# Attention with squared ReLU, then a feed-forward block, on one core: the first q and k in fp32 on SyncE's queue with a cast on chip, a TensorE warm-up, batch 1's first transposes on ScalarE, and batch 1's centering per feature block from PSUM

## The chip, the cores and the metric

The kernel runs on one core of one Trainium2 chip. The metric is the device time of one execution in microseconds (us). Most executions of one kernel repeat within 0.3%, but the times of this kernel and its variants fall into groups about 1.2 us (0.2%) apart, and telling these groups apart is half of this study. "Clock" is the share of TensorE's full clock that the chip granted, as the profile records it; a half-clock window is a stretch of 3.413 us (or two of them) at a clock of 0.5. All runs quoted are of the state "fast", or single runs whose state can't be told ("unknown", said where it is so).

Engines: PE = TensorE matmul, PEld = its weight loads, DVE = VectorE, ACT = ScalarE, POOL = GpSimd, SP = SyncE.

## The reference, cut to what matters

```python
# q, k, v: (batch 8, heads 12, seq 448, head_dim 64), fp32
scores = q @ k.T / sqrt(64)                       # per batch and head
attn   = maximum(scores, 0) ** 2 / 448
x      = (attn @ v), heads joined: (8, 448, 768)
# feed-forward with a layer norm ahead of it
xn  = (x - mean) / sqrt(var + 1e-6) * g_ln        # per row of 768
out = x + maximum(xn @ w_ch1, 0) @ w_ch2          # 768 -> 3072 -> 768
```

There is no softmax, so a score tile passes through three engines: TensorE makes it (called QK below), ScalarE or VectorE applies scale and ReLU, VectorE (or Pool) squares it, TensorE multiplies it with v (called AV).

## The kernel before: the parts that the change and the argument touch

Heads are taken in pairs of pairs: `n` counts groups of four heads ("pair n" in the texts), three of them (`NPER`) for each batch, and seven score tiles (`J`) in each. The kernel is emitted by a list scheduler that runs at build time: every piece of work is an `Op` with a guessed cost, and the guesses decide in which order each engine gets its instructions. On the chip the order of each queue is fixed. Loads go through Pool's software queue and are cast from fp32 to bf16 on the way:

```python
    nc.vector.memset(ones, 1.0 / d_model)
    ...
    with nc.allow_non_contiguous_dma(reason="768 gains, once"):
        nc.sync.dma_start(g_sb, moe_g_ln.rearrange("(ko kp) -> kp ko", kp=P))   # first of all loads

    def load_qk_rows(b, n):
        for t, src in enumerate((q, k)):
            ...
                nc.gpsimd.dma_start(stage[b][:, t, n::NPER, :], rows[:, n::NPER, :])
    ...
    with tc.manual_schedule():
        load_qk_rows(0, 0)
        ops["ident"] = R.add("POOL", 1300.0, lambda eng: make_identity(nc, identity), key=-1.0)
        load_qk_rows(0, 1)
        load_v(0)
        load_qk_rows(0, 2)
        load_qk_rows(1, 0)
        load_w1(0, 4)
        # ... the rest of batch 1 and of the weights
```

Batch 0 and 1 turn q and k by TensorE transposes into PSUM (the memory that matmuls write) and copy them to SBUF (the memory that matmuls read). In batch 0 each of q and k is one copy; batch 1's are one instruction of 1792 columns, on whichever engine the scheduler finds free:

```python
    def att_T(n):
        ...
        ev = R.add(("DVE", "ACT"), (1100.0, 1700.0), lambda eng: copy(
            eng, qkT[b][:, :, pn::NPER, :], st[0].rearrange("p t (j c) -> p t j c", c=P)), [op], key=0.01 * n - 0.008)
```

A score tile lives in a ring of nine buffers (`N_AT = 9`), which is freed tile by tile by AV. The squares are separate `Op`s for VectorE or Pool. When all three pairs of batch 0 are through AV, the means are taken by matmuls with a matrix of ones, and the first feed-forward can start after centering (VectorE) and gains (ScalarE), block by block:

```python
        mean_part(0)
        mean_part(1)
        mean_part(2)
        center(0)
        ...
        ffn_1_pair(0)
```

Batch 1 is centered otherwise: ScalarE copies the mean from PSUM to SBUF first, then four wide subtractions, then six gains, and only then does its first feed-forward matmul start.

## Time and profile before

| | before |
|---|---|
| time, median of six runs | 545.84 us (545.78 to 547.07) |
| PE busy of the profiled span (544.2 us) | 97% |
| PE busy in the first 5 us; first transposes | 0; at 5.40 us |
| first ReLU on ScalarE | 8.88 us |
| VectorE and ScalarE busy from 8.25 to 31 us (22.75 us) | 20.32 and 18.93 us |
| first AV matmul of pair 0 | 15.12 us |
| first subtraction of batch 0's centering | 30.79 us |

The head of the kernel, up to batch 0's centering, is the only place where PE waits for long.

The page of the kernel before (span; busy time and share of each engine):

```profile
span 544.2 us, 9868 instructions
PE 528.4 (97%) x4207; PEld 286.2 (53%) x4207; DVE 285.9 (53%) x494; ACT 227.8 (42%) x376; POOL 115.0 (21%) x133
```

The chain of waits of the kernel before, in order of time, its longer pieces up to 12 us (start, length, what the chain went through):

```profile
2.11 4.42 DMA t<-in_k_dram
6.57 0.97 PE ps L401 x16
7.57 0.63 DVE t L414
8.25 0.61 PE sc L466 x4
8.88 0.93 ACT a L475
9.85 0.58 PE sc L466 x3
10.44 1.34 PE ps L401 x49
```

The head begins with a load, and what follows is slow: four QK matmuls take 0.61 us here and 0.38 us later, which is TensorE at half clock.

The busy times in two stretches of the kernel before (busy time and count of each engine; then granted clock, DMA share, GB/s):

```profile
0.00:5.00 5.00, 0.00 (x0) 0.00 (x0) 0.22 (x2) 1.49 (x2) 3.88 (x11) 1.00 0.51 55
8.25:31.00 22.75, 18.51 (x365) 11.05 (x366) 20.32 (x37) 18.93 (x27) 12.20 (x16) 1.00 1.26 204
```

Five us with nothing on PE, then 22.75 us in which VectorE and ScalarE are both nearly full. The clock column says 1.00 although TensorE was cold: a record of the clock exists only from the first change on, here at 12.7 us, and time ahead of it counts as full.

The timeline of the kernel before (start, busy time, engine, line, operation; in brackets the idle time ahead and what ended it):

```profile
10.64 0.61 DVE L484 TENSOR_TENSOR a<-a 128x896 bf16<-128x896 bf16 x1
...
13.81 0.67 POOL L314 DMA_DIRECT2D v_t<-in_v_dram  x1 [1.35 <-DMA v_t<-in_v_dram]
...
15.12 1.52 PE L519 MATMUL ps<-a,v_t 64*64 64x448 bf16 x28
...
30.79 0.55 DVE L722 TENSOR_TENSOR a<-xT_e,ps 128x384 bf16<-128x384 bf16 x1
```

The first square is at 10.64. v comes in two halves, and AV needs both; "v" below is the second. It has landed by 13.81 (Pool's next load of v waited for it), 1.3 us before AV uses it. So v is early enough here, by a little.

### The profile page before, as it was taken

What the parts mean: (1) busy time and instruction counts of PE and PEld (TensorE: products, weight loads), DVE (VectorE), ACT (ScalarE), POOL (GpSimd) and SP (SyncE); (2) the same over time, 40 slices, a digit from 0 to 9 for tenths busy, and PEclk for the clock granted to TensorE, in tenths of its full rate; (3) what the DMA queues carried; (4) which work ended last, traced back from release to release, by engine and by line L of the source; (5) the groups of instructions that cost most, each with busy time, mean ns of one, the idle gap of its engine ahead of it and who ended that gap; (6) DMA issues with size and microseconds to landing.
All of it is one profiled execution on the core that took longest, in us unless ns stands there. A gap on an engine that the chain in (4) does not pass through costs nothing.

```text
span 544.2 us, 9868 instructions
## 1 busy us (share of the span) xinstructions
PE 528.4 (97%) x4207; PEld 286.2 (53%) x4207; DVE 285.9 (53%) x494; ACT 227.8 (42%) x376; POOL 115.0 (21%) x133
## 2 busy tenths in 40 slices
PE   4889999999999999999999999999999999999996
PEld 3444455555554455554555455555555555555563
DVE  3996566427864466834467355853456535540011
ACT  3976621115325653556124653265422554044200
POOL 7511700041270123410152120600210102100000
PEclk9999999999999999999999999999999999999999
DMA  9999999997199404990169601993023100510022
GB/s 144 205 200 180 211 170 145 158 149 143 41 157 149 69 1 83 160 158 1 31 87 183 117 1 34 167 145 55 2 51 82 30 0 1 96 50 1 1 58 59
DMA packets 141611, 51.36 MB, mean 94 GB/s; under 512 B 121728, under 2 KB 137344, under 8 KB 141568
## 3 DMA queue, kind: packets, MB, share of 16 engines
q0 software_dynamic: 81616, 25.96, 48.7%
q1 hardware_dynamic: 55472, 13.97, 19.7%
q10 hardware_dynamic: 4480, 10.82, 7.2%
q8 instruction: 33, 0.54, 0.4%
q14 instruction: 10, 0.08, 0.0%
HBM read 51.91 MB, written 11.01 MB: 116 GB/s over the span
## 4 chain that ended last, share of the span: by engine, by line
PE 94%; DVE 3%; ACT 1%; DMA 1%; issue 0%; POOL 0%; ACTq 0%; POOLq 0%
PE o_ps L838 40%; PE ps L782 40%; PE sc L466 6%; PE ps L519 5%; DVE a L484 1%; PE ps L401 1%; DMA t<-in_k_dram 1%; ACT a L710 1%; DVE t L414 1%; ACT a L475 1%; DVE a L477 0%; PE slot L681 0%; DVE xT_e L534 0%; DVE o_t L852 0%; ACT xT_e L532 0%
## 5 line engine op out<-in xcount | busy, mean ns | idle before, releaser
L782 PE MATMUL ps<-a,w 128*128 128x448 bf16 x1140 | 221.5, 353 | 0.0
L838 PE MATMUL o_ps<-w,h 128*128 128x384 bf16 x1200 | 199.7, 326 | 0.0
L782 PEld LDWEIGHTS <-w 128*128 128x128 bf16 x1140 | 108.8, 98 | 108.8 <-issue 10.6
L838 PEld LDWEIGHTS <-h 128*128 128x128 bf16 x1200 | 116.1, 98 | 81.5 <-issue 5.5
L475 ACT ACTIVATE a<-sc 128x896 bf16<-128x896 f32 x109 | 96.7, 925 | 93.2 <-PE sc L466 89.4
L797 ACT ACTIVATE h<-ps 128x448 bf16<-128x448 f32 (+1 forms) x161 | 85.1, 529 | 106.4 <-PE ps L782 105.9
L477 DVE TENSOR_SCALAR a<-sc 128x896 bf16<-128x896 f32 x59 | 64.1, 1087 | 108.4 <-PE sc L466 108.3
L484 DVE TENSOR_TENSOR a<-a 128x896 bf16<-128x896 bf16 x168 | 105.9, 669 | 3.6 <-ACT a L475 3.4
L852 DVE SCALAR_TENSOR_TENSOR o_t<-o_ps,r_t,a 128x384 f32<-128x384 f32 x56 | 34.4, 615 | 106.8 <-PE o_ps L838 106.5
L466 PE MATMUL sc<-t 64*64 64x448 bf16 x672 | 48.5, 365 | 3.5 <-ACT a L475 2.1
L519 PE MATMUL ps<-a,v_t 64*64 64x448 bf16 x672 | 37.8, 351 | 0.9 <-DVE xT_left L534 0.4
L710 ACT ACTIVATE a<-a,g_sb 128x448 bf16<-128x448 bf16 x38 | 22.3, 657 | 26.0 <-DVE a L703 21.6
L466 PEld LDWEIGHTS <-t 64*64 64x64 bf16 x672 | 18.0, 107 | 26.2 <-issue 19.6
L519 PEld LDWEIGHTS <-v_t 64*64 64x64 bf16 x672 | 19.9, 107 | 15.2 <-issue 4.0
L330 POOL DMA_DIRECT2D t<-in_q_dram x12 | 19.3, 1773 | 30.0 <-DMA t<-t 28.4
L604 POOL TENSOR_TENSOR sum_t<-sum_t,xT_o 128x384 f32<-128x384 f32 x7 | 6.4, 913 | 87.3 <-ACT xT_o L532 74.2
L838 PE MATMUL o_ps<-w,t 128*128 128x384 bf16 x144 | 23.9, 326 | 0.0
L330 POOL DMA_DIRECT2D t<-in_k_dram x12 | 23.7, 2527 | 0.0
L604 POOL TENSOR_TENSOR sum_t<-sum_t,xT_e 128x384 f32<-128x384 f32 x6 | 5.5, 912 | 81.1 <-ACT xT_e L532 76.0
L314 POOL DMA_DIRECT2D v_t<-in_v_dram x16 | 17.9, 1495 | 14.6 <-PE ps L782 6.6
L602 POOL TENSOR_TENSOR sum_t<-xT_o 128x384 f32<-128x384 bf16 x4 | 3.6, 910 | 80.9 <-DVE a L484 66.0
L838 PEld LDWEIGHTS <-t 128*128 128x128 bf16 x144 | 13.9, 98 | 9.8 <-issue 0.7
(60 smaller groups left out, 216.7 us busy)
## 6 DMA issues: line engine op xcount, KB each, us to landing
out_dram<-o_t ACTq DMA_DIRECT2D x54, 192.0 KB, 2.9
v_t<-in_v_dram POOLq DMA_DIRECT2D x16, 336.0 KB, 17.0
w<-in_moe_w_ch_dram POOLq DMA_DIRECT2D x4, 1152.0 KB, 41.8
t<-in_q_dram POOLq DMA_DIRECT2D x12, 336.0 KB, 7.6
t<-in_k_dram POOLq DMA_DIRECT2D x12, 336.0 KB, 11.7
w<-in_moe_w_ch_dram POOLq DMA_DIRECT2D x4, 768.0 KB, 15.7
w<-in_moe_w_ch_dram POOLq DMA_DIRECT2D x1, 1536.0 KB, 29.7
t<-in_q_dram POOLq DMA_DIRECT2D x6, 224.0 KB, 8.7
```

Source lines behind the costliest of these rows:

```text
L314: nc.gpsimd.dma_start(vt[b][half * T:(half + 1) * T], v[b, half * 6:half * 6 + 6].rearrange("h (p j) d -> p h (j d)", j=J))
L330: nc.gpsimd.dma_start(stage[b][half * T:(half + 1) * T, t].rearrange("p j (h d) -> p j h d", d=D), src[b, half * 6:half * 6 + 6].rearrange ...
L466: nc.tensor.matmul(sc[rows_of(half), r, :S], qkT[b][rows_of(r), 1, s * NPER + pn, rows_of(half)], qT[:, :, pn, rows_of(half)], start=True, ...
L475: nc.scalar.activation(attn[n, s], st[0][:, :, :S], Act.Relu, scale=rc2)
L477: nc.vector.tensor_scalar(attn[n, s], st[0][:, :, :S], rc2, 0.0, op0=Alu.mult, op1=Alu.max)
L484: nc.vector.tensor_mul(attn[n, s], attn[n, s], attn[n, s])
L519: nc.tensor.matmul(av_st[n][half][rows_of(hh)], vt[b][rows_of(half), 2 * pn + hh, s * D:(s + 1) * D], attn[n, s][rows_of(half), hh, :], st ...
L710: nc.scalar.mul(o, o, g_sb[:, ki:ki + 1])
L782: nc.tensor.matmul(ps, w1[:, ki, ni * P:(ni + 1) * P], xc[b][:, ki, :], start=(i == 0), stop=(i == K1 - 1))
L797: nc.scalar.activation(o, st[0][:, c], Act.Relu)
L838: nc.tensor.matmul(o_st["ps"], stat(ki), w2[:, ki, j * hd:(j + 1) * hd], start=(ki == 0), stop=(ki == K2 - 1))
L852: nc.vector.scalar_tensor_tensor(o_st[u, m][:, j * hd:(j + 1) * hd], ps, rstd[b][:, ri:ri + 1], xm[u, m][:, j * hd:(j + 1) * hd], op0=Alu. ...
```

## The change

The intent: start the head sooner and keep TensorE warm. Six things change (the code is cut; "..." marks what is left out).

1. The first q and k come over SyncE's hardware queue in three pieces (q, three sevenths of k, the rest of k), as fp32, and are cast on VectorE or ScalarE. The 768 gains, which led all loads, now follow these pieces.
2. 36 dummy matmuls warm TensorE up while it waits.
3. Batch 1's first transposes (pair 3) are copied by two instructions of 896 columns, on ScalarE only.
4. The mean matmuls enter the stream of AV pieces, so that pairs 0 and 1 are summed before pair 2 is evacuated; squares of batch 1 are held until batch 0 is centered.
5. Batch 1 is centered block by block from PSUM like batch 0, and its first feed-forward is cut into six parts.
6. The scheduler's bookkeeping follows (`flat`, `ahead`, `hold`).

```diff
+    FIRST = ((0, 0, J), (1, 0, 3), (1, 3, J))
+
+    def load_first():
+
+        raw = {}
+        ops["qk_ld", 0, 0] = []
+        for i, (t, j0, j1) in enumerate(FIRST):
+            cols = slice(j0 * D, j1 * D)
+            ... # i == 0: raw[0] is an fp32 view of a buffer that batch 1 uses later
+                nc.sync.dma_start(raw[0][:, t, :, cols], rows[:, 0::NPER, cols])
+            ld = R.add("SP", 480.0, emit, [], key=float(i), load=(2 * P, 22.0 + 7.0 * (j1 - j0)))
+
+            def cast(eng, t=t, cols=cols):
+                copy(eng, stage[0][:, t, 0::NPER, cols], raw[0][:, t, :, cols])
+            ops["qk_ld", 0, 0].append(
+                R.add(("DVE", "ACT"), (100.0 + 67.0 * (j1 - j0), 200.0 + 107.0 * (j1 - j0)), cast, [ld], key=-3.0))
 ...
+        if pn == 0:
+            ev = None
+            for t in range(2):
+                ev = R.add("ACT", 940.0, lambda eng, t=t: copy(
+                    eng, qkT[b][:, t, pn::NPER, :], st[0][:, t].rearrange("p (j c) -> p j c", c=P)), [op, ev], key=0.01 * n - 0.008)
+        else:
             ev = R.add(("DVE", "ACT"), (1100.0, 1700.0), ...)      # one copy, either engine
 ...
-        if n == NPER and s < 3:
+        if n == NPER and ("xc", 0) not in ops:
             held.append(add_square)
 ...
-        if b > 0:
+        if b > 1:
             sv = R.add("ACT", 560.0, save, [op, free], key=-2.0)   # mean to SBUF
 ...
-        if b == 0:
+        if b < 2:
             for ki in [pn + NPER * h for pn in range(NPER) for h in range(2)]:
                 ... # subtract one block from PSUM, then its gain
 ...
+        deps = f1_deps(b, ni)
+        for part in [[x] for x in k] if (b, ni) == (1, 0) else [k]:
+            op = R.pe(1135.0 / K1 * len(part), lambda eng, part=part: emit(eng, part), deps)
+            deps = [ops["xc", b][min(part[0][0] + 1, K1 - 1)]]
 ...
-        load_qk_rows(0, 0)
-        ops["ident"] = R.add("POOL", 1300.0, lambda eng: make_identity(nc, identity), key=-1.0)
+        ops["ident"] = R.add("POOL", 1300.0, lambda eng: make_identity(nc, identity), key=-2.0)
+        load_first()
+
+        def warm_up(eng):
+            ps = ps_s.tile([P, 2, 512], fp32, tag="s")
+            for i in range(N_WARM):                                # 36
+                nc.tensor.matmul(ps[:, 0, :P], ones, ones, start=True, stop=True)
+        slot_use(R.pe(N_WARM * 107.0, warm_up, []))
+
+        def gains(eng):
+            with nc.allow_non_contiguous_dma(reason="768 gains, once"):
+                nc.sync.dma_start(g_sb, moe_g_ln.rearrange("(ko kp) -> kp ko", kp=P))
+        R.add("SP", 480.0, gains, [], key=2.0, load=(6 * P, 32.0))
         load_qk_rows(0, 1)
         load_v(0)
 ...
+        av_stream += [("M", n) for n in range(NPER)]
-        mean_part(0)
-        mean_part(1)
-        mean_part(2)
         center(0)
```

Below, 1 and 2 are called the **front part**, 3 to 5 the **back part**.

## The prediction

> **What bounds it now.** TensorE. The page gives PE 97% busy of 544.2 us, and the chain of waits is 94% PE; from 37 us to 540 us it is an almost unbroken run of feed-forward and attention matmuls, so nothing there can be won. The head is different. By the busy time in stretches, PE is idle 5.4 us at the start and, in all, about 11 of the first 40 us. The chain of waits names why: 2.11 to 6.53 us the DMA of the first k (issue to landing 4.4 us), then cold transposes (0.97 us), the DVE copy (0.63), a cold QK (0.61), first ReLU at 8.88. From 8.25 to 31 us DVE is busy 20.3 and ACT 18.9 of 22.75 us: that stage is bound by the two together. Then come batch 0's centering and gains (31.5 to 35.2, six ACT gains of 0.667).
>
> **What the change does, step by step.**
> 1. First q/k on SyncE's queue. The gains load there moved its first packet at 1.9 us, against 3.75 us for the software queue's first q (DMA share in stretches). The Trainium skill, "DMA: Bandwidth & Descriptors", Specifications, also gives SyncE's path the shorter first byte (0.6 against 1 us); the trace shows a larger difference, since Pool's issue and start are in it. A pair's load took 1.15 us from landing to landing; so estimated landings are q 3.7, k's first part 4.2, k's rest 5. Added: casts, estimated 0.3 to 0.6 us each from the 0.62 us copy of as many elements, on idle DVE and ACT. Ready to transpose at about 4.5.
> 2. Warm-up. The Trainium skill, "TensorE: Matmul & The Clock Gate", Part 1, says PE runs at half clock until some 3.4 us of activity. The trace agrees: 51 transposes took 1.60 us at 10.2, 53 took 1.01 at 17.9; four QK took 0.59 at 9.9 and 0.38 at 13.3. 36 warm-up matmuls, at about 0.1 us each an estimated 3.9 us, end near 4.9, so they may hold up the first transposes by 0.3 us, but return some 0.7 us on the first chain.
>    Together: first QK at about 6.6 instead of 8.25, first ReLU at about 7.0 instead of 8.88. Later loads also come about 1.3 us sooner (the gains' 784 tiny packets, about 0.4 us of DMA time, now lie in their way); v may then limit attention of pair 0, so 1.5 of the 1.9 us should survive.
> 3. Batch 1's first transposes: 1.08 us leaves saturated DVE, two copies (1.9 us in all, estimated) go to ACT, which idled 1.5 us there. Mean matmuls of pairs 0 and 1 run before pair 2's evacuation is done, squares are held: about 0.6 us.
> 4. Batch 1's centering by block from PSUM: drops the 0.53 us save. PE did not idle at that point before (67 to 75 us), so about 0.
>
> Sum: about 2.4 us, all in the head, all on the critical path, carried unchanged to the end.
>
> **Predicted: 543.4 us**, 80% range 541.6 to 545.2. Faster by over 2%: 0.005; within 2%: 0.99; slower by over 2%: 0.005.
>
> **Right or wrong.** Right: first ReLU at 6.7 to 7.3 us; QK matmuls near 0.38 per four from the start; gains of batch 0 start about 2.3 us sooner; from there to the end as long as before. Wrong: first ReLU early but centering no earlier (then v's landing, or DVE plus ACT, took it back); cold QK after the warm-up; SyncE's load landing after 4.5; a PE gap near batch 1's first feed-forward.
>
> **What would spoil it.** Three SyncE loads competing with Pool's loads; ACT's extra 0.8 us delaying ReLUs; the warm-up ending late; the split first feed-forward stalling PE in order on ACT's or DVE's gains.

## The result, and the profile after

| | before | after |
|---|---|---|
| time, median of six runs | 545.84 us (545.78 to 547.07) | 547.17 us (545.97 to 547.40) |
| ratio after to before, 95% interval | | 1.0017 (1.0004 to 1.003) |
| of the six runs, above 547 us | 1 | 5 |
| mean granted clock over the runs | 1.000 (profiled run) | 0.992 to 0.994 in the five, 0.997 in the other |
| first ReLU (profiled run) | 8.88 us | 8.63 us |
| first subtraction of batch 0 (profiled run) | 30.79 us | 29.70 us |

A ratio is the mean time of one kernel's fast runs over that of the other's fast runs of the same rounds, so it isn't quite the ratio of the medians. Inside 2% the two are the same kernel. But the prediction was 543.4 us, 2.4 us of gain, and 1.3 us of loss came. The profiled run is the one run of the six that came out at 545.97 us, so its trace shows the better case, and the slow case had to be looked for.

The page of the kernel after:

```profile
span 544.0 us, 9973 instructions
PE 532.3 (98%) x4243; PEld 288.9 (53%) x4243; DVE 284.6 (52%) x499; ACT 231.0 (42%) x382; POOL 115.3 (21%) x132
```

The timeline of the kernel after, same columns as before:

```profile
1.09 4.02 PE L1115 MATMUL ps<-ones 128*128 128x128 bf16 x36 [1.09 <-DVE ones L280]
...
2.27 0.47 SPq L1120 DMA_DIRECT2D g_sb<-in_moe_g_ln_dram  x1
...
4.24 0.99 DVE L354 CAST t<-f 128x896 bf16<-128x896 f32 x2 [3.21 <-DMA f<-in_q_dram]
...
7.27 0.62 ACT L352 CAST t<-f 128x512 bf16<-128x512 f32 x1 [5.04 <-DMA f<-in_k_dram]
...
7.94 0.38 PE L459 MATMUL ps<-identity,t 64*64 64x64 bf16 x12 [1.99 <-ACT t L352]
...
8.63 2.54 ACT L539 ACTIVATE a<-sc 128x896 bf16<-128x896 f32 x3 [0.74 <-PE sc L530]
...
11.51 2.22 DVE L548 TENSOR_TENSOR a<-a 128x896 bf16<-128x896 bf16 x4
...
13.85 0.94 PE L583 MATMUL ps<-a,v_t 64*64 64x448 bf16 x14 [0.15 <-DMA v_t<-in_v_dram]
...
29.70 0.55 DVE L785 TENSOR_TENSOR a<-xT_e,ps 128x384 bf16<-128x384 bf16 x1 [0.96 <-PE ps L643]
```

Read it from the top. The warm-up ran from 1.09 to 5.1 us. q was on chip at 4.24 and was cast, and k's first piece after it; that is 1.2 us sooner than q before. But ScalarE sat until 7.27 for k's rest, and PE sat 1.99 us (5.95 to 7.94) until it was cast. The first three QK tiles need only k's first piece. They stand behind the transposes of k's rest in PE's queue, so cutting k in two didn't bring the first QK forward. The first square is at 11.51, later than the 10.64 of before, and v is there at 13.85, no sooner than before (Pool's next load of v, which waited for it, starts at 14.09; before, at 13.81).

The chain of waits of the kernel after, its longer pieces up to 14 us:

```profile
2.29 7.63 DMA t<-in_k_dram
9.97 0.84 PE ps L459 x23
10.97 0.62 DVE t L354
11.59 2.14 DVE a L548 x4
```

In this run the head no longer hangs on the first k but on the k of pair 1, which Pool's queue delivered at 9.97.

The busy times of the kernel after by stretch (last three columns: clock, DMA share, GB/s). The two stretches are windows of the clock record, 3.413 us each:

```profile
5.30:8.71 3.41, 1.42 (x68) 1.11 (x62) 1.18 (x3) 0.70 (x2) 1.85 (x3) 1.00 1.13 135
8.71:12.12 3.41, 3.17 (x74) 2.27 (x69) 1.91 (x5) 3.21 (x4) 1.72 (x3) 0.50 1.28 197
```

The warm-up did wake TensorE (full clock from 5.3 us, against 12.7 us before). Then PE was busy only 1.42 of 3.41 us, the 1.99 us wait being in it, and the next window ran at half clock.

This gave the theories that the experiments were to part:

- **A, the clock.** The warm-up wakes TensorE early; it then idles on late loads and is throttled again. How many half-clock windows fall on busy time decides the run.
- **V, the first v.** The head has to wait for v at 13.4 to 14.5 us, which no part of the change brings forward; an earlier first ReLU is lost there.
- **O, VectorE's order** (came up late). Pair 0's squares stand behind pair 1's copies in VectorE's queue.
- Rivals: **B**, the loss lies behind the head. **C**, the warm-up helps, and the back part costs. **D**, VectorE and ScalarE alone bound the head. **E**, the spread is the DMA's landing times, not the clock.

### The profile page after: what moved, and what is told of

Same layout as the page of the kernel before. It is cut to its first block, busy times and chain, and to the rows that moved or that the text cites. A ratio compares the mean times of both kernels' runs of the same rounds, so it can differ in the third digit from the quotient of the medians.

```text
span 544.0 us, 9973 instructions
## 1 busy us (share of the span) xinstructions
PE 532.3 (98%) x4243; PEld 288.9 (53%) x4243; DVE 284.6 (52%) x499; ACT 231.0 (42%) x382; POOL 115.3 (21%) x132
## 4 chain that ended last, share of the span: by engine, by line
PE 93%; DVE 3%; DMA 1%; ACT 1%; issue 0%; POOL 0%; POOLq 0%
PE o_ps L908 41%; PE ps L851 40%; PE sc L530 6%; PE ps L583 5%; DVE a L548 2%; DMA t<-in_k_dram 1%; ACT a L773 1%; PE ps L459 1%; DVE a L541 0%; DVE t L354 0%; PE slot L744 0%; PE ps L641 0%; DVE xT_e L354 0%; POOL t L322 0%; DVE o_t L922 0%
## 5 line engine op out<-in xcount | busy, mean ns | idle before, releaser
L541 DVE TENSOR_SCALAR a<-sc 128x896 bf16<-128x896 f32 x60 | 65.3, 1088 | 107.7 <-PE sc L530 107.6
L548 DVE TENSOR_TENSOR a<-a 128x896 bf16<-128x896 bf16 x167 | 104.8, 668 | 3.4 <-ACT a L539 3.3
L583 PE MATMUL ps<-a,v_t 64*64 64x448 bf16 x672 | 39.0, 351 | 1.9 <-DVE a L548 0.8
L773 ACT ACTIVATE a<-a,g_sb 128x448 bf16<-128x448 bf16 x40 | 23.6, 657 | 25.9 <-DVE a L766 24.9
```

Of the source, the lines that this page charges most:

```text
L541: nc.vector.tensor_scalar(attn[n, s], st[0][:, :, :S], rc2, 0.0, op0=Alu.mult, op1=Alu.max)
L548: nc.vector.tensor_mul(attn[n, s], attn[n, s], attn[n, s])
L583: nc.tensor.matmul(av_st[n][half][rows_of(hh)], vt[b][rows_of(half), 2 * pn + hh, s * D:(s + 1) * D], attn[n, s][rows_of(half), hh, :], st ...
L773: nc.scalar.mul(o, o, g_sb[:, ki:ki + 1])
```

## The experiments

Eighteen runs were made, in six groups; each group had one chip and its own runs of the kernel before (group medians 546.05 to 546.24 us). a1, c4 and d1 are the change again, e2 is d2 again, and b1 turned out to be the change again as well. All gave correct results. The kernel before has a slower group too: 12 of its 60 runs in these groups took more than 546.6 us, as one of six did at first. No trace of one was kept, so that group stays unexplained. "First subtraction" is that of batch 0's centering in the traced run.

| run | what | first ReLU | first subtraction | half clock in the trace, after the first full clock and before 540 | time, median (range) |
|---|---|---|---|---|---|
| before | | 8.88 | 30.79 | cold to 12.7 | 545.84 (545.78 to 547.07) |
| after | the change | 8.63 | 29.70 | 8.71 to 12.12 | 547.17 (545.97 to 547.40) |
| a1 | the change again | 7.65 | 29.59 | none | 545.70 (one run, state unknown) |
| c4 | the change again | 7.34 | 29.10 | none | 545.23 (one run, state unknown) |
| d1 | the change again | 8.93 | 30.54 | 13.55 to 16.96 | 546.43 (545.55 to 546.64) |
| a2 | no warm-up | 7.88 | 31.22 | cold to 19.8 | 546.58 (545.45 to 547.36) |
| a3 | dummy matmuls, order changed | 8.58 | 32.15 | 14.96 to 18.37 | 547.21 (546.75 to 548.41) |
| b3 | the same, and before AV | 8.44 | 31.42 | none | 547.39 (547.05 to 547.71) |
| c1 | dummy matmuls, order kept | 7.50 | 29.90 | none | 545.79 (545.55 to 546.04) |
| b1 | meant: gains loaded late; ran as the change | 7.60 | 28.77 | none | 545.96 (544.85 to 546.86) |
| c2 | as c1, with 20 for 30 | 7.55 | 30.63 | 12.31 to 15.72 | 545.58 (545.23 to 547.45) |
| b2 | v ahead of pair 1 | 7.64 | 32.27 | 13.55 to 20.37 | 548.74 (548.27 to 549.28) |
| f1 | squares ahead of pair 1's copies | 7.24 | 29.87 | 15.06 to 18.47 | 546.45 (546.00 to 547.36) |
| a4 | back part alone | 9.06 | 29.31 | cold to 11.5 | 544.99 (544.94 to 545.12) |
| b4 | back part without batch 1's centering | 8.83 | 29.07 | cold to 11.3 | 545.27 (545.22 to 545.39) |
| d3 | back part without ScalarE's copies | 8.79 | 31.70 | cold to 18.1 | 547.20 (545.99 to 547.60) |
| c3 | back part and warm-up | 8.55 | 29.54 | 9.34 to 12.75 | 544.66 (543.80 to 545.18) |
| d2 | c3 and 20 dummy matmuls | 8.44 | 28.06 | none | 544.16 (543.69 to 546.53) |
| e2 | d2 again | 8.65 | 29.00 | none | 544.17 (543.63 to 546.51) |
| e1 | d2 without ScalarE's copies | 8.82 | 29.72 | none | 545.04 (544.69 to 545.41) |

### The front and the back part, apart: a4, b4

a4 takes the front part out: first q and k by Pool, gains first, no warm-up.

```diff
-        ops["ident"] = R.add("POOL", 1300.0, ..., key=-2.0)
-        load_first()
+        load_qk_rows(0, 0)
+        ops["ident"] = R.add("POOL", 1300.0, ..., key=-1.0)
-        slot_use(R.pe(N_WARM * 107.0, warm_up, []))
-        R.add("SP", 480.0, gains, [], key=2.0, load=(6 * P, 32.0))      # back to the start of the program
```

> Only the back part of the change: first q/k by the Pool queue as before, no warm-up, gains loaded first as before; batch 1's first transposes on ScalarE, the mean matmuls in the stream, squares held, batch 1's centering by block stay. Theory A: this part is harmless and gains 0.4 to 0.9 us: about 545.2 us, first ReLU at 8.9, batch 0's gains on ScalarE at about 30.8. Rival C (the back part costs, by the split feed-forward or ScalarE's extra copies): 546 us or more.

Measured: 544.99 us, five runs within 0.18 us, 1.1 us below the 546.10 of the kernel before beside it (ratio 0.9982, 0.9969 to 0.9994). The first ReLU is at 9.06, as late as ever, and yet batch 0 is centered sooner than in the profiled run of the change, whose first ReLU was 0.4 us earlier. The timeline of a4:

```profile
14.93 1.52 PE L585 MATMUL ps<-a,v_t 64*64 64x448 bf16 x28
...
29.31 0.56 DVE L787 TENSOR_TENSOR a<-xT_e,ps 128x384 bf16<-128x384 bf16 x1 [1.19 <-PE ps L645]
```

AV runs as one piece of 28 here; no v is waited for. So the back part carries a gain, and the front part, put on top of it, won 0.1 us in the best of the change's 19 runs (544.85) and lost 2.2 us in its median of the first measurement. Rival C falls.

b4 is a4 with batch 1 centered as before:

```diff
-        if b < 2:          # center block by block from PSUM
+        if b == 0:
 ...
-        if b > 1:          # copy the mean to SBUF first
+        if b > 0:
 ...                         # and the orders that follow from it
-        for part in [[x] for x in k] if (b, ni) == (1, 0) else [k]:
+        for part in [[x] for x in k] if (b, ni) == (1, 99) else [k]:
```

> The back part alone (as a4_old_head) but with batch 1 centered as in the kernel before. My prediction costed step 4 at about 0: then this run equals a4_old_head, 545.0 us within 0.2. If the centering by block is what won a4's 1 us, this run falls back to about 545.9; if it costs, this run is below 544.8.

Measured: 545.27 us against a4's 544.99, in another group; the kernel before was 546.07 and 546.10 in the two. So the centering by block is worth 0.2 to 0.3 us, nearly the 0 that was predicted. (Both figures compare two groups, and b4's traced run, with its first subtraction at 29.07 against a4's 29.31, is no guide here: batch 1 is centered some 37 us later.)

### The change again, for its slow runs: a1, c4, d1

> The changed kernel unaltered, for a second trace, because five of its six timed runs took 547.1 to 547.4 us at a mean granted clock of 0.992 to 0.994, and the profiled one 545.97 at 0.997. Theory A (the warm-up wakes PE early, PE then idles on the late first k and is throttled again): about 547.2 us, clock about 0.993, and the windows view shows about 6.8 us of half clock after 5 us, all before 20 us; batch 0's gains on ScalarE start at about 31.6 instead of 30.4. Rival B (the 1.2 us lies elsewhere, in the weights' loads or in batch 1's centering): the first 31 us agree with the profiled run within 0.3 us and the difference appears later.

> The changed kernel unaltered once more, to catch a trace of its frequent slow execution (547.2 us). Theory A: a half-clock window or two within 8 to 20 us, the first attention times v matmuls and the transposes of pair 2 at half speed, batch 0's gains on ScalarE start at 31.5 to 32 instead of 30.3, the rest as before. Rival B: gains at 30.3 and the loss after it. If it falls into the 545.8 us state it tells nothing new.

> The changed kernel unaltered, timed five times beside its variants. If theory A holds, the times fall in two groups, near 545.2 to 546.0 and near 547.2, the second at a mean granted clock of 0.995 or less (half-clock windows beside the last one), and a trace of the second group has batch 0's gains on ScalarE at 31.3 to 32 instead of 29.8 to 30.4. If all five are near 545.5 here, the 547.2 group belongs to the circumstances of the first measurement. Rival B: a slow run whose gains start at 30.3.

a1 and c4 each fell in the better state (545.70 and 545.23 us). Both show what the front part does when nothing goes wrong: ReLU at 7.65 and 7.34, 1.2 to 1.5 us sooner than before. And both show PE waiting for v afterwards, 1.78 and 0.97 us. The timelines of a1 and of c4:

```profile
14.23 0.94 PE L583 MATMUL ps<-a,v_t 64*64 64x448 bf16 x14 [1.78 <-DMA v_t<-in_v_dram]
...
29.59 0.55 DVE L785 TENSOR_TENSOR a<-xT_e,ps 128x384 bf16<-128x384 bf16 x1 [0.96 <-PE ps L643]
```

```profile
13.74 0.94 PE L583 MATMUL ps<-a,v_t 64*64 64x448 bf16 x14 [0.97 <-DMA v_t<-in_v_dram]
...
29.10 0.55 DVE L785 TENSOR_TENSOR a<-xT_e,ps 128x384 bf16<-128x384 bf16 x1 [0.95 <-PE ps L643]
```

The traced run of d1 took 546.64 us and is the slow case that was wanted. The timeline of d1, and two windows of its clock:

```profile
14.24 1.70 PE L583 MATMUL ps<-a,v_t 64*64 64x448 bf16 x14 [0.50 <-DMA v_t<-in_v_dram]
...
30.54 0.56 DVE L785 TENSOR_TENSOR a<-xT_e,ps 128x384 bf16<-128x384 bf16 x1 [0.96 <-PE ps L643]
```

```profile
10.13:13.55 3.42, 2.03 (x40) 0.70 (x34) 3.33 (x7) 3.42 (x5) 1.29 (x2) 1.00 1.26 199
13.55:16.96 3.41, 2.91 (x34) 1.42 (x36) 2.80 (x5) 1.77 (x3) 2.05 (x3) 0.50 1.26 204
```

PE was busy 2.03 of 3.42 us, with three waits of 0.43 us for ScalarE to free score buffers; the window after it was at half clock, with the wait for v in it, just where the held-up AV and QK had to be caught up: the same 14 matmuls took 1.70 us instead of 0.94, and ScalarE and VectorE, both nearly full in the window before (3.42 and 3.33 us), fell to 1.77 and 2.80 us. a1 is the run to compare with, since its v came at the same time (14.23): batch 0's centering came 0.95 us later in d1 (30.54 against 29.59), and the time was 0.94 us longer (546.64 against 545.70). Against c4 the two differences are 1.44 and 1.41 us, but there v, too, was 0.50 us sooner (13.74). Theory A holds for this slow run, and rival B falls for it: what was lost was lost by 31 us and carried to the end unchanged.

One thing stays open. The first six runs had five at 547.1 to 547.4 us with a mean clock of 0.992 to 0.994. One half-clock window is worth 3.413 x 0.5 / 544 = 0.0031, and a half-clock stretch after the last matmul (from 541.0 us in c4) another 0.0020; so 0.993 would be two windows in the head, if none lies elsewhere. The thirteen later runs of the same kernel (a1, c4, d1 and, as it turned out, b1), on four chips, were 544.85 to 546.86 us, and no trace of a run with two windows was caught. Nor does the mean clock fix the time: a run of b1 had 0.993 and took 545.97 us.

### Without the warm-up: a2

```diff
-        slot_use(R.pe(N_WARM * 107.0, warm_up, []))
```

> The 36 warm-up matmuls removed, all else as in the change. Theory A: there is nothing to throttle again, the clock record reads 1.000 as in the kernel before, PE simply stays cold until about 13 us, most runs fall near 545.8 us (545.3 to 546.2) and the 547.2 group disappears or becomes rare. Rival C (the warm-up helps and something else in the change costs): runs get slower, 547.5 us or more.

A miss for the expectation: 546.58 us, spread from 545.45 to 547.36. The first ReLU was still early (7.88). But its traced run, the 547.36, was cold until 19.8 us: PE waited 1.17 us for v until 14.5, was busy 2.75, 2.91 and 2.24 us in three windows, and was released only after one in which it was busy throughout. Its first 14 AV matmuls after that wait took 1.70 us, as in d1. So an early start without the warm-up is hurt in the same way. Its mean clock is given as 1.000: without a first record, cold time counts as full.

### Keeping TensorE busy: a3, b3, c1

a3 puts 36 dummy matmuls where PE waits for k's rest; b3 also 36 ahead of the first AV.

```diff
+                if n == 0 and j0 > 0:
+                    def keep(eng):
+                        ps = ps_s.tile([P, 2, 512], fp32, tag="s")
+                        for _ in range(36):
+                            nc.tensor.matmul(ps[:, 0, :P], ones, ones, start=True, stop=True)
+                    slot_use(R.pe(36 * 56.0, keep, []))
```

> 36 more dummy matmuls (about 2 us) between the transposes of k's first part and those of its second, where PE idled 2 us waiting for the load. Theory A: PE is never throttled again, clock 0.999 or more, four QK take 0.38 us from the start, batch 0's gains start at about 29.8 us, all runs lie near 545.3 us (544.8 to 545.8). Rival B: clock rises but the time stays split between 546 and 547.2.

> The change with 36 dummy matmuls while PE waits for k's rest and 36 more just ahead of the first attention times v matmul, where PE waits for v. Loads are not touched. Theory A (the slow runs are those in which PE, idle over v, is throttled for the catch-up): no half-clock window after 6 us, all five runs within 0.5 us of each other, near 545.7 us. Rival E (the slow runs come from the DMA's landing times, not from the clock): the spread of 1.5 us stays although the clock stays full.

Both misses in the time: 547.21 and 547.39 us. a3's clock stayed full from 4.7 to 15.0 us and then fell for a window, after PE had been busy 1.14 of 3.41 us, waiting for squares and for v. b3's stayed full from 3.8 us until after the last matmul, and its six runs lay within 0.66 us. So the spread went with the clock, as theory A has it, but the whole was 1.6 us slower. The cause is in the edit: the dummy matmuls were given a cost in the build-time schedule and took a PSUM buffer out of turn, so that everything behind them was emitted in another order. c1 does it properly, at no cost in the schedule, 14 and 30 of them, written to PSUM where nothing is read yet:

```diff
+                    if n == 0 and j0 > 0:
+                        for _ in range(14):
+                            nc.tensor.matmul(late_fill[0][:, 0, :P], ones, ones, start=True, stop=True)
                     one(t, st[t], j0, j1)
 ...
+                if n == 0:                      # the first AV of pair 0
+                    for _ in range(30):
+                        nc.tensor.matmul(av_st[0][0][:, :P], ones, ones, start=True, stop=True)
```

> The change with 14 dummy matmuls before the transposes of k's rest and 30 before the first attention times v matmul, this time at no cost in the build-time schedule, so that every other instruction keeps its order (in a3 and b3 the order of the rest had changed as well). Theory A (clock): no half-clock window after about 6 us, all runs within 0.4 us, near 545.7 us, which is the change's best; the 547.2 group is gone. Rival E (the spread is DMA landing times): still 545.7 to 547.4.

Measured as theory A expects: 545.79 us, five runs within 0.49 us, no half-clock window in the head. The loads' landing was not touched, and none of the five runs is in the slow group, so E isn't what makes that group (it has a part in the rest of the spread, see b1). It is still no better than the kernel before (ratio 0.9993, 0.9979 to 1.0006): with a steady clock the medians differ by 0.4 us (546.15 to 545.79), where the back part alone was worth 1.1.

### The first v and the gains: b1, c2, b2

b1 was meant to issue the gains' load only after v has landed:

```diff
-        R.add("SP", 480.0, gains, [], key=2.0, load=(6 * P, 32.0))
         load_qk_rows(0, 1)
         load_v(0)
         load_qk_rows(0, 2)
         load_qk_rows(1, 0)
+        R.add("SP", 480.0, gains, ops["v_ld", 0], key=2.0, load=(6 * P, 32.0))
```

> The gains' load (768 elements of 4 bytes) is issued on SyncE only after the first v has landed; all else as in the change. Theory V (the first v's landing, at 13.8 to 14.2 us however early the first ReLU is, is what the head waits for; the gains' tiny packets run between 3.4 and 10.9 us among q, k and v): v lands 0.5 to 0.9 us earlier (about 13.3), batch 0's gains on ScalarE start at about 29.8 in a run without a late cold window, and the best runs come to about 545.0 us; the spread by the clock stays. Rival D (DVE and ScalarE together bound the head, v is chance): v earlier, but gains at 30.3 as before, time unchanged.

The timeline of b1:

```profile
2.27 0.47 SPq L1124 DMA_DIRECT2D g_sb<-in_moe_g_ln_dram  x1
...
13.35 0.94 PE L583 MATMUL ps<-a,v_t 64*64 64x448 bf16 x14 [0.77 <-DMA v_t<-in_v_dram]
...
28.77 0.55 DVE L785 TENSOR_TENSOR a<-xT_e,ps 128x384 bf16<-128x384 bf16 x1 [0.95 <-PE ps L643]
```

The first line tells that the edit didn't do what it was meant to: the gains' load is issued at 2.27 us, as in the change. The dependency stands in the build-time schedule alone and only fixes an order; no load stood between the two places in SyncE's queue, so the program that ran is the change, with the same instructions in the same order on VectorE, ScalarE, Pool and SyncE. c2 and b2 issue the gains at 2.27 as well. So what the gains' packets cost the other loads was never tested. (They take 0.7 to 0.8 us of all DMA engines in the traces of the change, from 3 to 12 us among q, k and v; before, they took 0.41 us and were done by 3.0.)

As one more repeat, b1 settles something else. Four traces have the change's order and a full clock from 6 us on:

| trace | pair 1's k used from | AV goes on with v at | first subtraction | time of the traced run |
|---|---|---|---|---|
| b1 | 9.36 | 13.35 | 28.77 | 544.85 |
| c4 | 9.55 | 13.74 | 29.10 | 545.23 |
| a1 | 9.23 | 14.23 | 29.59 | 545.70 |
| c1 (with dummy matmuls) | 9.24 | 14.54 | 29.90 | 546.04 |

The subtraction follows v by 15.36 to 15.42 us in all four, and the time follows the subtraction; pair 1's k doesn't order them. So in this order, with a full clock, v's landing sets the centering, as theory V has it. Rival D falls for the change, since VectorE and ScalarE had the same work in runs 1.1 us apart. And E is right in part: v's landing, which moves from run to run for a reason that no run shows, is worth up to 1.2 us of time. No experiment moved v alone.

c2, meant as b1 with 14 and 20 dummy matmuls, is c1 with 20 for 30 ahead of AV, on the same chip.

> The same with the gains loaded after the first v (as b1), 14 and 20 dummy matmuls. Theory V plus theory A: v lands near 13.3 us, batch 0's gains start on ScalarE near 29.5, all runs near 544.8 us (544.5 to 545.2): below the kernel before and as good as or better than a4_old_head. Rival E: 544.8 to 546.9 as in b1.

A miss: 545.58 us, and one run at 547.45, which is the traced one: half clock from 12.31 to 15.72 after a window with 1.86 us of PE work. The twenty are no cause of that, since they start at 12.60; run at half clock they took 2.31 us and held AV until 14.85, though v was there by 13.74 (Pool's next load of v). So filling costs time itself when the clock falls all the same: the centering is at 30.63, against 29.90 in c1.

b2 has v loaded ahead of pair 1's q and k (and, like b1, the gains' load unmoved in fact):

```diff
-        load_qk_rows(0, 1)
         load_v(0)
+        load_qk_rows(0, 1)
```

> As b1_gains_late, and the first v is loaded ahead of q and k of pair 1. Theory V: v lands at about 11.5 us, PE no longer sits waiting for it, no cold window later than about 13 us, spread shrinks, and the time comes to 544.0 to 545.0 us. Rival D: v early but the time stays at 545.5 to 547; or the wait is only moved to pair 1's q and k (landing about 13), which would show as a PE wait on them of 1 us or more.

The worst run of all, 548.74 us. The wait only moved: PE stood at 11.1 and 13.1 us for pair 1's q (0.48 us) and k (1.36 us), whose transposes come ahead of AV in its queue, and TensorE was at half clock from 13.55 to 20.37. That was the rival outcome that the expectation names.

### VectorE's order: f1

By then the timelines of the better runs showed another fact. In the kernel before, and in a4, VectorE does one ReLU and one square ahead of pair 1's copies. In the change all of pair 0's squares come after those copies, which wait for pair 1's loads. So the first square is at 10.77 in c4, as late as before, and VectorE idled 2.0 us waiting for those copies between 7.6 and 10.2. f1 moves only this:

```diff
-                               st[t].rearrange("p (j c) -> p j c", c=P)[:, j0:j1]), [op], key=-1.0)
+                               st[t].rearrange("p (j c) -> p j c", c=P)[:, j0:j1]),
+                           [op] + ([ops["at", 0, 1]] if n == 1 else []), key=-1.0)
```

> The change with one dependency more in the build-time schedule: the copies of pair 1's transposed q and k come after the second square of pair 0, so that VectorE's queue holds one ReLU and three squares ahead of them (in the change all of them stand behind those copies, which wait for pair 1's loads until 9.7 to 11 us, and the first square starts at 10.8 however early the first ReLU is). The loads are not touched. Theory O (VectorE's order, not v, gives the early start back): first square at about 9.2, batch 0's gains on ScalarE at 28.6 to 29.3 in a run without a cold window, best runs at 544.0 to 544.8 us. Theory V (v's landing at 13.7 to 14.2): first square early, gains still at 29.8 to 30.4, best runs 545.2 to 545.7 as in the change. The clock's spread stays either way.

The timeline of f1 (VectorE, and PE's wait):

```profile
8.63 1.68 DVE L549 TENSOR_TENSOR a<-a 128x896 bf16<-128x896 bf16 x3
...
14.03 0.94 PE L584 MATMUL ps<-a,v_t 64*64 64x448 bf16 x14 [0.85 <-DMA v_t<-in_v_dram]
...
16.69 0.56 DVE L354 CAST xT_e<-ps 128x384 bf16<-128x384 f32 x1 [1.87 <-PE ps L584]
```

The squares came 2.1 us sooner than in c4 (8.63 against 10.77), and nothing was won: 546.45 us (546.00 to 547.36), centering at 29.87. VectorE ran out of work and idled 1.87 us until AV was through; AV had waited for v until 14.03 and then ran in a half-clock window. All five runs have a clock of 0.992 to 0.997, so a half-clock window is in the measured times and the size of theory O alone stays unmeasured. But the trace shows that PE still waits for v (0.64 and 0.85 us) when VectorE's order no longer holds the squares back. That there are two limits at about the same time, v and VectorE's queue behind pair 1's loads, is likely and not shown.

### The back part with a warm TensorE: c3, d2, e2, and step 3 apart: d3, e1

c3 adds the 36 warm-up matmuls, and nothing else of the front part, to a4.

> a4_old_head plus the 36 warm-up matmuls alone, the first q and k by the Pool queue. PE idles from about 5 to 5.4 us only. Theory V (the head waits for v, at 13.8 us): first ReLU 0.4 to 0.6 us sooner (8.5), first attention times v matmul at 14.2 to 14.8, 0 to 0.6 us gained: 544.5 to 545.1 us. Theory A adds a risk of single runs 1 us slower where PE is throttled between 9 and 16 us. If the warm-up itself is what costs, 546 us or more.

544.66 us (543.80 to 545.18), ratio 0.9971 (0.9958 to 0.9983). The traced run, 545.18, again has a half-clock window (9.34 to 12.75) after one with 1.84 us of PE work; no trace was kept of the runs at 543.8 and 543.9.

d2 fills the two idle places ahead of 8.2 us:

```diff
+                    if n == 0 and t == 1:       # ahead of the first k's transposes
+                        for _ in range(10):
+                            nc.tensor.matmul(late_fill[0][:, 0, :P], ones, ones, start=True, stop=True)
 ...
+            if (n, s) == (0, 0):                # ahead of the first QK
+                for _ in range(10):
+                    nc.tensor.matmul(late_fill[0][:, 0, :P], ones, ones, start=True, stop=True)
```

> c3_back_warm with 10 dummy matmuls before the transposes of the first k and 10 before the first QK, at no cost in the build-time schedule, so that PE does not idle between 5 and 8.2 us. c3's runs were 543.8 to 545.2, the slower with half clock from 9.6 to 13.0. Theory A: no such window, all runs near 543.9 (543.6 to 544.4), faster than both kernels. Rival E: still 543.8 to 545.2.

> d2_back_steady once more, beside e1 on the same chip: most runs 543.7 to 544.4 us, at most one or two slower by 1 to 2.5 us at a clock of 0.997 or less.

d2: 544.16 us, five of six runs at 543.69 to 544.36 and one at 546.53 with a clock of 0.993. e2, on another chip: 544.17 us, five at 543.63 to 544.63 and one at 546.51 (0.994). Both ratios are 0.9967 (0.9952 to 0.9982 and 0.9983). This is the best version found: 2.0 us below the kernel before, 3.0 below the first measurement of the change, and not quite free of the bad window.

d3 and e1 take ScalarE's two copies away again, from a4 and from d2:

```diff
-        if pn == 0:                # batch 1's first transposes: two copies, ScalarE
+        if pn == 9:                # never: one copy on either engine, as before
```

> a4_old_head with batch 1's first transposes copied by one instruction on either engine, as in the kernel before; the means in the stream and the held squares stay. My prediction gave the three together 0.6 us; a4 won 1.0 us. If ScalarE's copies are the larger part this run is at 545.6 us or more; if the means' order and the held squares are, it stays at 545.1 us or less.

> d2_back_steady with batch 1's first transposes copied as in the kernel before (one instruction on either engine). In d3 the same step was mixed with a TensorE that stayed cold until 18 us in the traced run; here the warm-up and the 20 dummy matmuls keep it warm. If ScalarE's two copies are worth the larger part of step 3 (0.5 us or more), the runs without a cold window lie at 544.5 to 545.2, against about 544.0 for e2 beside it; if they are worth nothing, both agree within 0.2 us and d3's 547.2 was the clock alone.

d3's 547.20 us mixes two things: its traced run was cold until 18.1 us. Why a4 was released by 11.5 us and d3 was not, with the same instructions until then and PE busy 2.9 and 2.8 us of the window, stays open. e1 beside e2, both with full clock, is clean. The timelines of e1 and of e2:

```profile
25.47 1.08 DVE L357 COPY t<-ps 128x1792 bf16<-128x1792 bf16 x1
...
29.72 0.55 DVE L794 TENSOR_TENSOR a<-xT_e,ps 128x384 bf16<-128x384 bf16 x1
```

```profile
25.87 1.71 ACT L355 COPY t<-ps 128x896 bf16<-128x896 bf16 x2
...
29.00 0.55 DVE L794 TENSOR_TENSOR a<-xT_e,ps 128x384 bf16<-128x384 bf16 x1 [1.19 <-PE ps L652]
```

In e1 VectorE spends 1.08 us on the copy just ahead of pair 2's last squares, which AV, the means and the centering wait for. In e2 ScalarE does it in 1.71 us at a time at which it has nothing else to do. The times: 545.04 us for e1, 544.11 for the mean of e2's five runs without the bad window; 0.9 us for this one step, and 0.7 at the first subtraction of the two traces.

## Why the prediction was wrong, point by point

- **What bounds the kernel, "carried unchanged to the end".** Right where two runs of one order are compared: what was won or lost was there at batch 0's centering and went to the end unchanged (d1 against a1: 0.95 us at the centering, 0.94 us in the time; b1 against a1: 0.82 and 0.85). Wrong between the change and the kernel before: c4's centering is 1.69 us sooner than before, its last matmul (ending at 538.53 against 539.83) 1.30, its time 0.85 (545.23 against 546.08 in the profiled run of before). From the last matmul's end to the end of the time it is 6.7 us in every trace of the change, 6.25 before, and 6.1 to 6.2 in a4, c3, d2, d3, e1 and e2 (b4's 6.8 is left out: its time and its profiled span lie further apart than in any other run). 0.3 us of the difference stand in the profile, in SyncE's waits at the program's end. They come with the first loads on SyncE and not with the warm-up (a2 has them, c3 hasn't); what in them does it wasn't tested.
- **Step 1, the first load and ReLU.** Half right. q was predicted to land at 3.7 and was cast from 4.24, k's rest at 5 and was cast from 5.6 or 5.7 (a1, c4) to 7.3 or 7.6 (profiled run, d1). The prediction's "three SyncE loads competing with Pool's loads" names what happened: in the profiled run 241 of the 256 packets of k's rest had started by 5.03 us, and the last fifteen came in small groups until 6.9, after Pool's queue had started at 4.7. The Trainium skill, "DMA: Bandwidth & Descriptors", section "Queues, rings and completion order", says that each DMA engine takes turns between its queues, one packet of several descriptors at a time; the late small groups fit that, but the turns themselves are not seen here, and in a1 all 256 had started by 5.0. And the prediction overlooked the order on PE: the early QK tiles stand behind k's rest. First ReLU: 7.0 predicted, 7.3 to 8.9 measured.
- **"Later loads also come about 1.3 us sooner", "1.5 of the 1.9 us should survive".** This is the step that failed. AV had v at 13.4 to 14.2 us in the five traces of the change; by the same mark, Pool's next load of v, v was there 0.2 us sooner (b1) to 0.7 us later (a1, d1) than before. The prediction had named v as a possible limit and charged it 0.4 us. Pool's queue, whose loads are of the same size as before less one pair, moved its first packet at 4.7 us instead of 2.8 (the prediction took this for 3.75), behind SyncE's loads; then it ran at 140 to 150 GB/s from 5 to 9 us, where before it had 191 from 4 to 8. Worked out from these rates, the slower stretch cost an estimated 1 us. The gains' packets, costed by the prediction at 0.4 us, took about 0.8 of it all; whether they are what slowed it was not tested (b1). The kernel before had 1.3 us of slack at v; the early start used it up and then waited, in PE for v (0.97 and 1.78 us) and in VectorE's queue for pair 1's copies. In the traces without a half-clock window the head gained 1.2, 1.7 and 2.0 us at the centering (a1, c4, b1), where the back part alone gains 1.5 (a4). So the front part's share there is -0.3 to 0.5 us, as v lands, and the program's end takes about 0.5 back.
- **Step 2, the warm-up.** The prediction counted what it gives (full clock from 3.8 to 6.7 us in every trace with it, against 11.3 to 19.8 without) and not what it risks. A TensorE woken at 5 us can be put back to half clock by its own waits, and the change had made it wait more for loads (the profiled run; in d1 the waits just ahead of the half-clock window were for ScalarE). One such window, on the catch-up after v, cost 0.9 us (d1 against a1). The prediction has "cold QK after the warm-up" as a sign of being wrong, but under "what would spoil it" only a warm-up that ends late.
- **Step 3, and 4 of the list above.** The mechanism was right, the size wrong: 0.6 us predicted for the transposes, the means and the held squares together. a4 won 1.1 us with the centering of batch 1, 0.8 without it (b4), and in the steady kernel ScalarE's copies alone are 0.9. The term was mis-sized because the 1.08 us on VectorE stood just ahead of the last square that the centering waits for, where it counted almost in full, while ScalarE's 1.71 us fell into idle time.
- **Batch 1's centering, "about 0".** Nearly right: 0.2 to 0.3 us (b4 against a4).
- **The sum.** 2.4 us of gain were predicted; about 1.1 came from the back part, about 0 from the front part in its good runs, and minus 0.9 for a half-clock window such as d1's in its bad ones. That the slow majority of the first measurement had such windows is inferred from its mean clock; none of those runs was traced.

## What to carry to other kernels

Before you start a stage sooner, look at its second input: in a pipeline that shares one DMA, an earlier first load is worth only as much as the slack of the next one that the stage meets (here v, with 1.3 us). Warming TensorE pays only if it's then kept busy, so treat a wait of a microsecond or two after the warm-up as a cost, and fill it, without letting the fill reorder anything or outlast the wait. Look into the trace whether an edit moved what it was meant to move: b1's didn't. And when times fall into groups, get a trace from each group before explaining any mean; the mean granted clock alone can mislead, since it counts the cold time ahead of the first record as full.

## What the Trainium skill lacked or had wrong

- "TensorE: Matmul & The Clock Gate", Part 1, tells of throttling after an idle window of about 3.4 us. Here no window was idle: TensorE fell to half clock after windows in which the profile counts 1.14, 1.42, 1.47, 1.79, 1.84, 1.86 and 2.03 us of PE work out of 3.41, and stayed at full clock after others with 1.80, 1.91, 1.93 and more. So waits that fill some 40 to 67% of a window were enough, though not always. The page tells of a clock that oscillates with frequent short idles, but gives no such measure.
- The same page says that one busy window releases the clock. Cold windows with 2.24, 2.48, 2.75, 2.79, 2.83, 2.88 and 2.91 us of PE work did not release it; others with 2.73, 2.84, 2.86, 2.87, 2.91 and up to 3.41 did. A kernel that works in gaps can stay cold for 20 us (a2) without being idle.
- No page says that the mean granted clock of a run counts the time ahead of the first clock record as full: a2 reads 1.000 and was cold until 19.8 us.
- "DMA: Bandwidth & Descriptors", Specifications, gives first bytes after about 0.6 us on SyncE's queue and 1 us on Pool's. From the start of the issue to the first packet the traces show 1.1 us (0.74 to 1.85) on SyncE; on Pool it was 1.6 us (1.25 to 2.82) in the kernel before and 3.2 us (1.44 to 4.65) when SyncE's loads were ahead of it.
- The same page doesn't tell what 4-byte packets cost when they run among other loads: the gains' packets took 0.41 us of all DMA engines when they ran ahead of the others and 0.7 to 0.8 us among q, k and v (about 8 and 15 ns each). What they cost those loads is not shown here.
